# First MLP with one block of 256 tokens, whose products take high and low parts side by side

## The chip, the core and the metric

The kernel runs on one core of a Trainium2 chip. The metric is the device time of one execution in microseconds. Before the change the median of three runs is 883.94 us (883.59 to 884.92). The engines are named as in the profile: PE is TensorE, and PEld its weight loads; DVE is VectorE, ACT is ScalarE, POOL is GpSimd, SP is the engine that issues most DMAs.

## What is computed

```python
def _attn_ref(q, k, v):                      # q, k, v: (4, 8, 576, 64)
    scores = scale * np.matmul(q, k.transpose(0, 1, 3, 2))
    Dmat = np.where(rel >= 0, gamma[:, None, None] ** rel[None, :, :], 0.0)
    return np.matmul(scores * Dmat[None, :, :, :], v)

def _moe_ref(x, w_in, w_out):                # x: (2304, 512), w_in: (512, 2048)
    h = x @ w_in
    g = h * (1.0 / (1.0 + np.exp(-1.702 * h)))
    return g @ w_out

def _moe2_ref(x, w_gate, w_val, w_out, rms_g):   # w_gate: (512, 1536)
    xn = x / np.sqrt(np.mean(x * x, axis=-1, keepdims=True) + 1e-06) * rms_g
    g = xn @ w_gate
    return (g * (1.0 / (1.0 + np.exp(-g))) * (xn @ w_val)) @ w_out
```

The attention's output, as 2304 rows of 512, goes through the first MLP and then through the second. All of it is float32.

## The kernel before

**Number format.** Each float32 operand of an MLP product is split into a high part, rounded to a format that PE takes in one pass, and a low part, the rest. A product is then three matmuls: high x high, high x low, low x high (`three`, lines 277 to 285). The high part comes from an ACT cast, the low part from a DVE (or POOL) subtraction. The weights arrive as float32; ACT rebuilds their words in two steps (lines 189 and 190), DVE joins them (line 243), and then they are split.

**Tiles.** The first MLP goes through the tokens in `BLOCKS`, 512, 384, 384, 512 and 512 of them, and in each block through 16 hidden slices `f` of 128. `m1_up(n, f)` multiplies the block's rows by slice f of `w_in`: four steps of 128 over the model width, three matmuls each, into one PSUM bank `h` of two. ACT takes gelu out of the bank (line 630) and rounds the high part (610), DVE subtracts for the low part (612). `m1_down(n, f)` multiplies the result by slice f of `w_out`, three matmuls for each of four `acc` banks, which collect over all f. Up runs two slices ahead of down (`LAG`).

**Output weights.** `w_rot(n, f)` makes the rounded halves of slice f of `w_out`, in a ring of three: an ACT cast (268) and a DVE subtraction (269), 128x512 whatever the block, while the float32 weights are kept; in block 1 it also stores them (`out_d`), and from slice 13 of block 1 on they are loaded again by a DMA that ACT issues.

**Attention between the products.** The rows of 128 tokens are a unit. Units 0 to 3 are done before the first product; the others run inside the MLP at slices written out in `at_steps`, a list of slices per block: `a_trans(u)` transposes q and k (line 364), and `a_both(u)` does the scores and key-value sums of unit u (396, 405) and the output products of unit u-1 (475). These output products take both `h` banks; ACT copies them out (484), DVE adds (488), and the rows are split by ACT (494) and POOL (495). `a_both(u)` also issues the loads of unit u+1 on SP. In a slice with `a_both`, the down product that is due runs right behind it, ahead of the slice's up product.

**Preparation.** From slice 11 of block 1 on, `make(k)` runs k steps of `prep` per slice: words, joins and splits of the second MLP's gate and value weights. The first two steps are the words of both (four ACT instructions), the next two their joins on DVE, then splits (872, 873), sums on POOL (845).

**Order.** Nothing is scheduled by a planner (`tc.manual_schedule()`): each engine's queue holds its instructions in the order in which this code calls them, each queue runs in order, and semaphores tie the queues.

Of the kernel before, what the change touches and what calls it, by code (L numbers as in the profile page):

```python
# [10 lines left out]
F32 = mybir.dt.float32  # L11
# [7 lines left out]

BLOCKS = (512, 384, 384, 512, 512)  # L20
BLOCKS2 = (768, 768, 768)
XB = 512
TH = 384
# [19 lines left out]
def kernel(  # L43
# [232 lines left out]

    def three(ps, lhs, rhs, first, last, more=False, swap=False):

        (lh, ll), (rh, rl) = lhs, rhs
        pairs = [(lh, rl), (ll, rh)]  # L280
        if swap:
            pairs.reverse()
        nc.tensor.matmul(ps, lh, rh, start=first, stop=False, skip_group_check=more)  # L283
        nc.tensor.matmul(ps, *pairs[0], start=False, stop=False, skip_group_check=more)  # L284
        nc.tensor.matmul(ps, *pairs[1], start=False, stop=last, skip_group_check=more)  # L285

# [70 lines left out]
    def a_trans(u, where):  # L357
# [146 lines left out]

    def wide_scores(u, where, amid=lambda: None):
        qT, kT = st[u]
# [10 lines left out]
        for j in range(2):  # L517
            nc.vector.tensor_tensor(
                out=r[j], in0=sc[j].rearrange("p (a c) -> p a c", c=2 * C),
                in1=wide_mask.unsqueeze(1).to_broadcast([128, HP, 2 * C]), op=ALU.mult,  # L520
            )
            if j == 0:
                amid()
        st[u] = qT, r
# [81 lines left out]
    def g_tile(c):  # L606
        return gp.tile([128, XB], F32, tag="g", name="g", bufs=2)[:, :c]

    def split_hidden(g, gh, gl, fill=lambda: None):
        nc.scalar.copy(out=gh, in_=g)  # L610
        fill()
        nc.vector.tensor_tensor(out=gl, in0=g, in1=gh.bitcast(F32), op=ALU.subtract)  # L612

    def proj(ps, key, f, x, c):
        wh, wl = W[key, f]
        xh, xl = x
        for kk in range(KD):
            three(
                ps,
                (wh[:, kk * 128:(kk + 1) * 128], wl[:, kk * 128:(kk + 1) * 128]),  # L620
                (xh[:, kk, :c], xl[:, kk, :c]),
                kk == 0, kk == KD - 1, swap=key == "in" and f == 0 and c == XB and x is xt.get(0),
            )

    def m1_up(n, f, fill, amid=lambda: None):
        c = BLOCKS[n]
        ps = ps_h.tile([128, XB], F32, tag="h", name="h")[:, :c]
        proj(ps, "in", f, xt[n], c)
        g = g_tile(c)
        nc.scalar.activation(out=g, in_=ps, func=AF.Gelu_apprx_sigmoid)  # L630
        amid()
        G[1, n, f] = hidden_parts(c)
        split_hidden(g, *G[1, n, f], fill)

    def m1_down(n, f):


        def piece(e):
            if f == 0 and e == 0:
                acc[n] = [ps_acc.tile([128, 512], F32, tag="acc", name="acc") for _ in range(4)]  # L640
            wh, wl = R["out", f]
            three(
                acc[n][e][:, :BLOCKS[n]],
                (wh[:, e * 128:(e + 1) * 128], wl[:, e * 128:(e + 1) * 128]),
                G[1, n, f], f == 0, f == NF1 - 1,
            )
            if f == NF1 - 1:
# [13 lines left out]
    def m1_end(n, e):  # L661
# [4 lines left out]
        y = halves([ends[n]], c)[0]  # L666
        (nc.vector.tensor_copy if e % 2 else nc.scalar.copy)(out=y[:, e % 2, :], in_=acc[n][e][:, :c])
        if e % 2:
# [115 lines left out]

    def beside_rows():
        return [t[:, :3, TH:] for t in block_tile(0)]

# [231 lines left out]
    with tc.manual_schedule():  # L1019
# [6 lines left out]
        def a_both(u, where):  # L1026
# [169 lines left out]
        (word, join, wh, wl), (word1, join1, wh1, wl1) = in_halves(0)  # L1196
        word()
        high()
        wide_scores(3, ACC, join)
        wh()  # L1200
        word1()
        low(engine=nc.gpsimd)
# [6 lines left out]
        high(slice(0, 2))  # L1209
        wl()  # L1210
        join1()
        low(slice(0, 2))
        (next_word, join, wh, next_wl), (word2, join2, wh2, wl2) = in_halves(1)
        next_word()
        wh1()
        to_conv.pop(0)
        scaled(1)
        spread_row(nc.gpsimd, qdec, qrow)
        high(slice(2, 4))
        low(slice(2, 4))  # L1220
        for u in range(4):
            a_free(u, "x")
        wl1()
        word2()
# [50 lines left out]
        for n in range(N1):  # L1275
# [19 lines left out]
            for f in range(NF1):  # L1295
# [26 lines left out]
                if (n, f) in ((2, 1), (3, 1), (3, 14)):  # L1322
                    sq = first_load(*{
                        (2, 1): (0, 0, beside_rows()), (3, 1): (0, 1, beside_rows()),
                        (3, 14): (1, 0, in_place(A_WIN)),
# [185 lines left out]
```

## Time and profile before

| | us |
|---|---|
| median of three runs (883.59 to 884.92) | 883.94 |
| the profiled execution | 884.29 |
| its span | 882.6 |
| PE busy | 874.7 |
| DVE busy | 516.1 |
| ACT busy | 382.2 |
| POOL busy | 92.5 |

The span runs from the first to the last instruction; 1.7 us of the profiled execution lie outside it. A busy PE is one that has matmuls in flight: they overlap, so how many it issues in a time is read from the distances of their starts.

### The profile page before, as it was taken

To read this page: it belongs to the slowest core of one execution; us is meant where nothing else is said; L and a number is where in the kernel's file an instruction comes from. 1 tells how busy PE (TensorE), PEld (TensorE's weight loads), DVE (VectorE), ACT (ScalarE), POOL (GpSimd) and SP (SyncE) were. 2 spreads that over 40 slices of the span, in tenths; PEclk is the share of its full clock that TensorE was granted. 3 is DMA by queue.
4 is the path that set the end of the run, shared out by engine and by line. 5 is a ranking of instruction groups with operands and counts; after the bars stand their busy time and mean duration, and the time that the engine had idled before them with its cause. 6 is when DMAs were issued, how large, how long until landed. Compare 5 with 4: busy or idle time off the path is not lost.

```text
span 882.6 us, 16195 instructions
## 1 busy us (share of the span) xinstructions
PE 874.7 (99%) x6176; PEld 789.3 (89%) x6176; DVE 516.1 (58%) x921; ACT 382.2 (43%) x766; POOL 92.5 (10%) x100
## 2 busy tenths in 40 slices
PE   8999999999999999999999999999999999999998
PEld 6788889999999888888889999999999999999997
DVE  4878754474574555756645567765575666333444
ACT  3776753365445554564463343334322215112222
POOL 5100111131232212311200000000000000000000
PEclk9999999999999999999999999999999999999999
DMA  9996444799779987897776676557655556555553
GB/s 209 252 291 197 135 159 159 212 319 317 233 247 316 292 254 237 274 390 262 258 281 219 215 241 209 167 167 267 211 156 158 152 157 224 163 159 157 166 168 107
DMA packets 153584, 193.26 MB, mean 219 GB/s; under 512 B 66656, under 2 KB 94564, under 8 KB 153508
## 3 DMA queue, kind: packets, MB, share of 16 engines
q1 hardware_dynamic: 144596, 164.83, 59.7%
q10 hardware_dynamic: 8688, 27.14, 9.3%
q8 instruction: 49, 0.80, 0.4%
q0 software_dynamic: 224, 0.27, 0.1%
q14 instruction: 27, 0.22, 0.1%
HBM read 149.99 MB, written 42.21 MB: 218 GB/s over the span
## 4 chain that ended last, share of the span: by engine, by line
PE 97%; SPq 1%; DMA 1%; ACT 0%; DVE 0%; issue 0%; DVEq 0%
PE h L285 17%; PE h L283 17%; PE h L284 17%; PE acc L283 11%; PE acc L284 11%; PE acc L285 11%; PE v L285 2%; PE v L284 2%; PE v L283 2%; PE at L475 1%; PE at L364 1%; SPq L339 1%; PE at L396 1%; PE at L405 1%; DMA sslots<-in_moe_w_in_dram 1%; DMA wslots<-in_q_dram 0%
## 5 line engine op out<-in xcount | busy, mean ns | idle before, releaser
L283 PE MATMUL h<-fast 128*128 128x384 f32 (+1 forms) x824 | 288.4, 350 | 0.2 <-ACT fast L589 0.2
L285 PE MATMUL h<-fast 128*128 128x384 f32 (+1 forms) x824 | 287.3, 349 | 0.0
L284 PE MATMUL h<-fast 128*128 128x384 f32 (+1 forms) x824 | 286.7, 348 | 0.1
L922 DVE TENSOR_TENSOR wslots<-h,wslots 128x384 f32<-128x384 f32 x180 | 100.1, 556 | 151.4 <-PE h L285 151.1
L283 PE MATMUL acc<-fast 128*128 128x512 f32 (+1 forms) x464 | 175.0, 377 | 0.0
L285 PE MATMUL acc<-fast 128*128 128x512 f32 (+1 forms) x464 | 174.4, 376 | 0.0
L284 PE MATMUL acc<-fast 128*128 128x512 f32 (+1 forms) x464 | 174.3, 376 | 0.0
L283 PEld LDWEIGHTS h<-fast 128*128 128x128 f32 x824 | 154.7, 188 | 9.9 <-ACT sslots L190 0.4
L284 PEld LDWEIGHTS h<-fast 128*128 128x128 f32 x824 | 154.8, 188 | 9.3 <-DVE fast L218 0.5
L285 PEld LDWEIGHTS h<-fast 128*128 128x128 f32 x824 | 154.6, 188 | 8.2 <-DVE fast L255 0.4
L612 DVE TENSOR_TENSOR fast<-g,fast 128x512 fp32r<-128x512 f32 (+1 forms) x80 | 54.4, 680 | 122.5 <-ACT fast L610 121.8
L955 ACT CAST fast<-g 128x384 fp32r<-128x384 f32 x36 | 18.5, 514 | 219.8 <-DVE g L925 219.8
L630 ACT ACTIVATE g<-h 128x512 f32<-128x512 f32 (+1 forms) x80 | 44.2, 553 | 136.0 <-PE h L285 132.9
L285 PEld LDWEIGHTS acc<-fast 128*128 128x128 f32 x464 | 87.1, 188 | 13.3
L283 PEld LDWEIGHTS acc<-fast 128*128 128x128 f32 x464 | 87.1, 188 | 12.7
L284 PEld LDWEIGHTS acc<-fast 128*128 128x128 f32 x464 | 87.1, 188 | 12.0
L873 DVE TENSOR_TENSOR wslots<-wslots 128x256 fp32r<-128x256 f32 x84 | 43.6, 554 | 15.1 <-ACT wslots L872 14.8
L845 POOL TENSOR_TENSOR wslots<-wslots 128x256 f32<-128x256 f32 x48 | 43.1, 918 | 75.5 <-DVE wslots L243 62.5
L610 ACT CAST fast<-g 128x512 fp32r<-128x512 f32 (+1 forms) x80 | 46.3, 578 | 2.5
L495 POOL TENSOR_TENSOR fast<-x,fast 128x512 fp32r<-128x512 f32 x14 | 18.7, 1339 | 225.6 <-ACT fast L494 225.6
L189 ACT ACTIVATE sslots<-sslots 128x512 f32<-128x512 f32 x56 | 37.8, 675 | 2.3 <-DMA sslots<-in_moe_w_out_dram 2.3
L190 ACT ACTIVATE sslots<-sslots 128x512 uint32<-128x512 uint8 x56 | 37.2, 664 | 0.0
(138 smaller groups left out, 871.0 us busy)
## 6 DMA issues: line engine op xcount, KB each, us to landing
fast<-up_d SPq DMA_DIRECT2D x252, 256.0 KB, 3.0
fast<-out_d ACTq DMA_DIRECT2D x51, 512.0 KB, 5.6
up_d<-wslots SPq DMA_DIRECT2D x84, 256.0 KB, 5.1
sslots<-in_moe_w_out_dram SPq DMA_DIRECT2D x19, 512.0 KB, 5.1
out_d<-fast SPq DMA_DIRECT2D x16, 512.0 KB, 3.7
sslots<-in_moe_w_in_dram SPq DMA_DIRECT2D x15, 512.0 KB, 5.3
sslots<-in_moe_w_val_dram SPq DMA_DIRECT2D x12, 512.0 KB, 6.5
sslots<-in_moe_w_gate_dram SPq DMA_DIRECT2D x11, 512.0 KB, 5.7
```

The costliest lines, as they stand in the source:

```text
L189: nc.scalar.activation(out=hi, in_=hi, func=AF.Prelu, scale=2.0 ** -112, alpha=-(2.0 ** 32))
L190: nc.scalar.activation(out=lo, in_=byte, func=AF.Copy, scale=1 / 32, bias=-31 / 64)
L283: nc.tensor.matmul(ps, lh, rh, start=first, stop=False, skip_group_check=more)
L284: nc.tensor.matmul(ps, *pairs[0], start=False, stop=False, skip_group_check=more)
L285: nc.tensor.matmul(ps, *pairs[1], start=False, stop=last, skip_group_check=more)
L495: nc.gpsimd.tensor_tensor(out=xl, in0=x, in1=xh.bitcast(F32), op=ALU.subtract)
L610: nc.scalar.copy(out=gh, in_=g)
L612: nc.vector.tensor_tensor(out=gl, in0=g, in1=gh.bitcast(F32), op=ALU.subtract)
L630: nc.scalar.activation(out=g, in_=ps, func=AF.Gelu_apprx_sigmoid)
L845: nc.gpsimd.tensor_tensor(out=o, in0=a, in1=b, op=op)
L873: nc.vector.tensor_tensor(out=wl.bitcast(F32R), in0=w, in1=wh, op=ALU.subtract)
L922: nc.vector.tensor_tensor(out=o, in0=a, in1=b, op=ALU.add)
```

## The change

Block 1 has 256 tokens and block 2 has 512. In a block of at most 256 tokens, a high weight part multiplies the rows' high and low parts in one matmul, 256 columns of each side by side in a bank, and the low weight part multiplies the high rows in a matmul of 256 columns (`two`). The two sides are then added: ACT copies the second out of PSUM and DVE adds the first (`joined_sides`), at each up product and at the block's end. `three` keeps one order of its parts; the first product of all has an order of its own, low rows last. Ahead of the first product, the words of the first input weights, their join and their halves are called at other places, and DVE makes qT of unit 3. The attention phases stand at other slices: block 0 holds six phases and block 1 eight, where it was eight and six. `make` runs 2 steps a slice in block 1 (4 before) and 3 in block 2 (2 before).

```diff
-BLOCKS = (512, 384, 384, 512, 512)
+BLOCKS = (512, 256, 512, 512, 512)
...
-            nc.scalar.copy(out=qT, in_=pt[0])
+            (nc.vector.tensor_copy if u == 3 else nc.scalar.copy)(out=qT, in_=pt[0])
...
+        if x is xt.get(0) and key == "in" and f == 0 and not begun:
+            begun.append(f)
+            order = [(kk + k, i, j) for kk in (0, 2) for k, i, j in (
+                (0, 0, 0), (0, 1, 0), (1, 0, 0), (1, 1, 0), (0, 0, 1), (1, 0, 1))]
+            for kk, i, j in order:
+                l, r = parts[kk]
+                nc.tensor.matmul(ps, l[i], r[j], start=(kk, i, j) == order[0], stop=(kk, i, j) == order[-1])
+            return
...
+    def both(at, k, c):
+        return fast[:, at:at + 2 * k * XB].rearrange("p (i k c) -> p k i c", i=2, k=k)[:, :, :, :c]
+
+    def two(bank, lhs, rhs, first, last):
+        c = bank.shape[1] // 2
+        (lh, ll), r = lhs, rhs
+        wide = bank.rearrange("p (i c) -> p i c", i=2)
+        if first:
+            nc.tensor.matmul(wide, lh, r, start=True, stop=False)
+        nc.tensor.matmul(wide[:, 0, :], ll, r[:, 0, :], start=False, stop=False)
+        if not first:
+            nc.tensor.matmul(wide, lh, r, start=False, stop=last)
+
+    def joined_sides(out, bank):
+        c = bank.shape[1] // 2
+        nc.scalar.copy(out=out, in_=bank[:, c:])
+        nc.vector.tensor_tensor(out=out, in0=bank[:, :c], in1=out, op=ALU.add)
...
+        if c <= XB // 2:
+            wh, wl = W["in", f]
+            rows_at = both(n % 2 * 2 * KD * XB, KD, c)
+            for kk in range(KD):
+                ks = slice(kk * 128, kk * 128 + 128)
+                two(ps, (wh[:, ks], wl[:, ks]), rows_at[:, kk], kk == 0, kk == KD - 1)
+            joined_sides(h, ps)
...
+            if BLOCKS[n] <= XB // 2:
+                two(acc[n][e], w, G[1, n, f], f == 0, f == NF1 - 1)
...
+        if c <= XB // 2:
+            joined_sides(y[:, e % 2, :], acc[n][e])
...
-            (2, 3, 4, 6, 8, 10, 12, 14),
-            (1, 3, 5, 7, 9, 10),
+            (2, 3, 4, 6, 9, 12),
+            (0, 2, 4, 6, 8, 10, 12, 14),
...
+        (word, join, wh, wl), (word1, join1, wh1, wl1) = in_halves(0)
+        word()
         a_trans(3, AT)
...
+        join()
         high()
-        wide_scores(3, ACC, join)
+        wide_scores(3, ACC)
         wh()
+        wl()
...
-                    make(2 if n == 2 else 3 if last and f > 5 else 4)
+                    make(2 if n == 1 else 3 if n == 2 or last and f > 5 else 4)
```

PE, block 1, a down product: `acc` are the four banks that collect over the slices, `fast` holds the split operands. Before, two of the four banks:

```order
L283 MATMUL acc_1511<-fast_88 128x384
L284 MATMUL acc_1511<-fast_88 128x384
L285 MATMUL acc_1511<-fast_88 128x384
L283 MATMUL acc_1512<-fast_88 128x384
L284 MATMUL acc_1512<-fast_88 128x384
L285 MATMUL acc_1512<-fast_88 128x384
```

Now, all four banks:

```order
L638 MATMUL acc_1472<-fast_88 128x256
L640 MATMUL acc_1472<-fast_88 128x512
L638 MATMUL acc_1473<-fast_88 128x256
L640 MATMUL acc_1473<-fast_88 128x512
L638 MATMUL acc_1474<-fast_88 128x256
L640 MATMUL acc_1474<-fast_88 128x512
L638 MATMUL acc_1475<-fast_88 128x256
L640 MATMUL acc_1475<-fast_88 128x512
```

Each bank takes two matmuls in place of three, one of them wider and one narrower.

ACT, block 1, from the last of the word instructions at slice 11 to the up product of slice 13 (`g` is the gelu tile, `at` the attention's banks). Before:

```order
L190 ACTIVATE sslots_93<-sslots_93 128x512
L268 CAST fast_88<-wslots_92 128x512
L630 ACTIVATE g_2107<-h_2094 128x384
L610 CAST fast_88<-g_2107 128x384
L872 CAST wslots_92<-wslots_92 128x256 x3
```

Now:

```order
L190 ACTIVATE sslots_93<-sslots_93 128x512
L268 CAST fast_88<-wslots_92 128x512
L368 COPY wslots_92<-at_1936 128x512
L644 COPY g_1949<-h_1948 128x256
L662 ACTIVATE g_1949<-g_1949 128x256
L605 CAST fast_88<-g_1949 128x256
```

The weight cast (268) still stands behind the words; behind it come the kT copy of a unit's transposes and the new copy out of `h`.

DVE, block 1, slices 12 to 14: 243 are the joins, 269 the weight subtraction, 410 (before: 413) the masks of an `a_both`. Before:

```order
L612 TENSOR_TENSOR fast_88<-g_2067,fast_88 128x384
L243 SCALAR_TENSOR_TENSOR wslots_92<-sslots_93 128x512 x2
L269 TENSOR_TENSOR fast_88<-wslots_92,fast_88 128x512
L612 TENSOR_TENSOR fast_88<-g_2107,fast_88 128x384
L873 TENSOR_TENSOR wslots_92<-wslots_92 128x256 x3
```

Now:

```order
L370 TENSOR_TENSOR wslots_92<-at_1935,qdec_102 128x512
L645 TENSOR_TENSOR g_1949<-h_1948,g_1949 128x256
L607 TENSOR_TENSOR fast_88<-g_1949,fast_88 128x256
L243 SCALAR_TENSOR_TENSOR wslots_92<-sslots_93 128x512 x2
L269 TENSOR_TENSOR fast_88<-wslots_92,fast_88 128x512
L645 TENSOR_TENSOR g_1980<-h_1979,g_1980 128x256
L607 TENSOR_TENSOR fast_88<-g_1980,fast_88 128x256
L910 TENSOR_TENSOR wslots_92<-wslots_92 128x256 x2
L410 TENSOR_TENSOR wslots_92<-at_2007,mask_98 128x4x64
L410 TENSOR_TENSOR wslots_92<-at_2008,mask_98 128x4x64
L485 TENSOR_TENSOR x_2069<-at_2043,x_2069 128x128
```

The sums out of `h` (645) stand in the same queue behind the joins and the weight subtraction, and an `a_both` follows in slice 14.

## Rows read from the trace of the kernel before

**Rows 1.** The page, part 1: busy us (share of span) xinstructions.

```profile
PE 874.7 (99%) x6176; PEld 789.3 (89%) x6176; DVE 516.1 (58%) x921; ACT 382.2 (43%) x766; POOL 92.5 (10%) x100
```

**Rows 2.** PE's waits, first and last of six: total us, times, longest.

```profile
PE heat L1106 <- DVE ones L1083: 1.1, 1, 1.1
...
PE h L283 <- ACT fast L589: 0.2, 1, 0.2
```

**Rows 3.** Timeline of PE, block 1: start us, duration us, instruction.

```profile
133.19 0.34 PE L285 MATMUL acc<-fast 128*128 128x384 f32 x1
...
135.76 0.34 PE L284 MATMUL acc<-fast 128*128 128x384 f32 x1
...
137.67 0.33 PE L283 MATMUL h<-fast 128*128 128x384 f32 x1
...
143.74 0.34 PE L285 MATMUL acc<-fast 128*128 128x384 f32 x1
...
144.96 0.34 PE L284 MATMUL h<-fast 128*128 128x384 f32 x1
```

**Rows 4.** Timeline of PE, block 3, 512 tokens.

```profile
295.87 0.39 PE L283 MATMUL h<-fast 128*128 128x512 f32 x1
...
303.80 0.39 PE L285 MATMUL acc<-fast 128*128 128x512 f32 x1
```

**Rows 5.** Groups by line and shape: xcount | busy us, mean ns | idle before.

```profile
L269 DVE TENSOR_TENSOR fast<-wslots,fast 128x512 fp32r<-128x512 f32 x26 | 22.1, 850 | 2.6 <-ACT fast L268 2.2
...
L484 ACT COPY x<-at 128x256 f32<-128x256 f32 x28 | 9.0, 375 | 26.4 <-PE at L475 26.4
...
L413 DVE TENSOR_TENSOR wslots<-at,mask 128x256 f32<-128x256 f32 x28 | 10.5, 418 | 8.9 <-PE at L405 8.9
...
L215 ACT CAST fast<-ww 128x256 fp32r<-128x256 f32 x4 | 1.5, 402 | 2.4 <-DVE ww L209 2.4
...
L243 DVE SCALAR_TENSOR_TENSOR wslots<-sslots 128x512 uint32<-128x512 uint32 x36 | 24.2, 684 | 2.5 <-ACT sslots L190 2.5
...
L189 ACT ACTIVATE sslots<-sslots 128x512 f32<-128x512 f32 x56 | 37.8, 675 | 2.3 <-DMA sslots<-in_moe_w_out_dram 2.3
```

**Rows 6.** Timelines of PE, ACT, DVE and POOL, block 1; [idle before <-releaser].

```profile
174.87 0.33 PE L283 MATMUL h<-fast 128*128 128x384 f32 x1
...
175.06 0.49 ACT L630 ACTIVATE g<-h 128x384 f32<-128x384 f32 x1 [3.65 <-PE h L285]
...
176.00 0.62 ACT L494 CAST fast<-x 128x512 fp32r<-128x512 f32 x1
...
178.09 0.67 ACT L189 ACTIVATE sslots<-sslots 128x512 f32<-128x512 f32 x1
...
180.32 0.63 ACT L268 CAST fast<-wslots 128x512 fp32r<-128x512 f32 x1
...
177.18 1.36 DVE L269 TENSOR_TENSOR fast<-wslots,fast 128x512 fp32r<-128x512 f32 x1 [0.48 <-ACT fast L268]
...
176.70 1.29 POOL L495 TENSOR_TENSOR fast<-x,fast 128x512 fp32r<-128x512 f32 x1 [12.62 <-ACT fast L494]
...
136.41 0.49 DVE L488 TENSOR_TENSOR x<-at,x 128x128 f32<-128x128 f32 x2 [1.00 <-ACT x L484]
```

**Rows 7.** DMA issues by line: xcount, KB each, median us to landing.

```profile
wslots<-in_q_dram SPq DMA_DIRECT2D x30, 128.0 KB, 4.4
```

**Rows 8.** Timelines of PE, ACT, DVE and SP's issues, start and block 0.

```profile
24.31 0.50 PE L283 MATMUL h<-fast 128*128 128x512 f32 x1 [0.16 <-ACT fast L589]
...
44.25 0.68 ACT L189 ACTIVATE sslots<-sslots 128x512 f32<-128x512 f32 x1 [2.28 <-DMA sslots<-in_moe_w_out_dram]
...
49.99 0.69 DVE L255 TENSOR_TENSOR fast<-ww,fast 128x512 fp32r<-128x512 f32 x1
...
50.10 0.47 PE L283 MATMUL h<-fast 128*128 128x512 f32 x1
...
33.20 4.79 SPq L339 DMA_DIRECT2D wslots<-in_q_dram  x2
```

More of the change, by code (lines that the diff above doesn't have):

```diff
@@ L275, in w_rot, with three @@
         R["out", f] = (wh, wl)
-    def three(ps, lhs, rhs, first, last, more=False, swap=False):
+    def three(ps, lhs, rhs, first, last, more=False):
         (lh, ll), (rh, rl) = lhs, rhs
-        pairs = [(lh, rl), (ll, rh)]
-        if swap:
-            pairs.reverse()
         nc.tensor.matmul(ps, lh, rh, start=first, stop=False, skip_group_check=more)
-        nc.tensor.matmul(ps, *pairs[0], start=False, stop=False, skip_group_check=more)
-        nc.tensor.matmul(ps, *pairs[1], start=False, stop=last, skip_group_check=more)
+        nc.tensor.matmul(ps, lh, rl, start=False, stop=False, skip_group_check=more)
+        nc.tensor.matmul(ps, ll, rh, start=False, stop=last, skip_group_check=more)
     C = 64
@@ L503, with wide_scores @@
     wide_mask = sp.tile([128, TH], F32, tag="norm", name="wide_mask", bufs=3)[:, :2 * C]
[L505 removed]
+    def wide_scores(u, where):
         qT, kT = st[u]
@@ L612, in split_hidden @@
         nc.vector.tensor_tensor(out=gl, in0=g, in1=gh.bitcast(F32), op=ALU.subtract)
+    begun = []
     def proj(ps, key, f, x, c):
@@ L616, in proj @@
         xh, xl = x
[L617 to L623, printed above, removed]
+        parts = [((wh[:, kk * 128:(kk + 1) * 128], wl[:, kk * 128:(kk + 1) * 128]), (xh[:, kk, :c], xl[:, kk, :c]))
+                 for kk in range(KD)]
+        if x is xt.get(0) and key == "in" and f == 0 and not begun:
[6 more added lines that the diff above has]
+            return
@@ new lines, in proj @@
+        for kk, (l, r) in enumerate(parts):
+            three(ps, l, r, kk == 0, kk == KD - 1)
+    def both(at, k, c):
[9 more added lines that the diff above has]
+            nc.tensor.matmul(wide, lh, r, start=False, stop=last)
@@ L631, in m1_up @@
         amid()
+        at = A_HID + n_hid[0] % 3 * 1024
         G[1, n, f] = hidden_parts(c)
         split_hidden(g, *G[1, n, f], fill)
+        if c <= XB // 2:
+            G[1, n, f] = both(at, 1, c)[:, 0]
     def m1_down(n, f):
@@ L640, in piece @@
                 acc[n] = [ps_acc.tile([128, 512], F32, tag="acc", name="acc") for _ in range(4)]
[L641 to L646, printed above, removed]
+            w = [t[:, e * 128:(e + 1) * 128] for t in R["out", f]]
+            if BLOCKS[n] <= XB // 2:
+                two(acc[n][e], w, G[1, n, f], f == 0, f == NF1 - 1)
+            else:
+                three(acc[n][e][:, :BLOCKS[n]], w, G[1, n, f], f == 0, f == NF1 - 1)
             if f == NF1 - 1:
@@ L666, in m1_end @@
         y = halves([ends[n]], c)[0]
-        (nc.vector.tensor_copy if e % 2 else nc.scalar.copy)(out=y[:, e % 2, :], in_=acc[n][e][:, :c])
+        if c <= XB // 2:
+            joined_sides(y[:, e % 2, :], acc[n][e])
+        else:
+            (nc.vector.tensor_copy if e % 2 else nc.scalar.copy)(out=y[:, e % 2, :], in_=acc[n][e][:, :c])
         if e % 2:
@@ L781, in norm_steps, with beside_rows @@
         ]
-    def beside_rows():
-        return [t[:, :3, TH:] for t in block_tile(0)]
+    def beside_rows(n):
+        return [t[:, :3, TH:] for t in block_tile(n)]
     def in_place(at):
```

24 lines of the change are left out of this document (11 added, 13 removed).

## The prediction

> **What bounds the kernel now.** The page's first part is read first: PE is busy for 99% of the span [rows 1]. PE's own waits come next: six in all, the longest 1.1 us, all before the first product of the MLP [rows 2]. So from the first product to the last, PE never stands still; its instructions, one after another, are the time. The change can gain only by giving PE less to issue, and it loses whatever makes PE wait, at once and in full.
>
> I call U(f) and D(f) the up and the down product of hidden slice f in token block 1, 16 slices in all. "Both" is one unit's attention scores with another's output, "trans" a unit's transposes.
>
> **Fewer matmuls.** Matmuls start at even distances: 36 of 384 columns from 137.67 to 143.74 us, 0.1734 us each [rows 3]; 36 of 512 columns from 295.87 to 303.80, 0.2266 each [rows 4]. The 128 columns between cost 0.0532, so 512 cost 0.2128, and 0.0138 of each matmul is independent of its width. Block 1 goes from 16 slices x 24 matmuls of 384 to 16 x 16, half of 512 and half of 256; block 2 goes from 384 matmuls of 384 to 384 of 512. The columns are the same in sum, 128 matmuls fall away: 128 x 0.0138 = **1.8 us saved**. A 256-column matmul would then start 0.2266 - 2 x 0.0532 = 0.120 after the one before. No row has one of this kind. Its upper bound is the 0.173 of the 384s [rows 3], should the loading of the next weights set the distance; that adds 128 x 0.053 = 6.8 us. Its lower bound is the columns alone, 0.106, another 1.8 saved. I take 0.120: the line through two widths already holds whatever a load of 128 columns costs in every matmul.
> The Trainium skill (TensorE: Matmul & The Clock Gate, Back-to-back issue gap) has another overhead: the columns at the full clock plus 2.5 ns. By it the saving would be 0.3 us, an estimate, and my sum 1.5 us higher; the distances of these rows exceed it, and they decide.
>
> **What the narrow block asks of the other engines.** U and D take 4 x (0.227 + 0.120) = 1.39 us each, where they took 2.08. Per slice the work behind them does not shrink alike: the rounding of the output weights stays 128x512 (ScalarE cast 0.62, VectorE subtract 0.69 to 1.36 [rows 5, 6]), and a ScalarE copy and a VectorE sum of 128x256 out of PSUM are new (0.38 and 0.42 by the nearest forms [rows 5]). The chain from U's end to its finished halves becomes: 0.19 until ScalarE starts (174.87 to 175.06 [rows 6]), copy 0.38, sum 0.42, gelu about 0.40, cast 0.40, subtract 0.42, some 2.3 us; before, 1.8. The bank of U is free only after the sum, so a VectorE queue that is late now holds PE directly: through the bank, through G and through the rounded weights. Also, block 1 now holds four trans and four boths, the last at slice 14, where block 1 had its last at slice 10.
>
> Costs of the attention to PE: both 133.19 to 135.76 less two distances = 2.22 us; trans 143.74 to 144.96 less two = 0.87 [rows 3]. They are moved, not added: nothing.
>
> **Where PE waits: slices 11 to 14**, counted from U(10)'s end as 0. PE wants U(11), D(9), trans, U(12), D(10), U(13), D(11) at 0, 1.39, 2.77, 3.65, 5.03, 6.42, 7.81, then the scores of the both at 9.2 and its output products at 10.3.
> - The other side: copy(10) 0.2, sum to 1.0, gelu, cast to 1.9, cast of the attention rows (0.62) to 2.4, weight cast(10) to 3.0. GpSimd's subtract of these rows (1.29 at 176.70) runs beside VectorE's weight subtract(10), which then takes 1.36, as at 177.18 [rows 6]: to 4.35. Sum(11) to 4.75, gelu and cast(11) to 5.6.
> - Here ScalarE has the four conversions of the first gate and value weights before the weight cast(11): 178.09 to 180.32, 2.23 us [rows 6]. Cast(11) 7.75 to 8.4, subtract(11) to 9.1. **D(11) wants it at 7.8: 1.3 us of wait.** In the kernel before, the same four stood there and slices were longer.
> - Then kT copy, copy(12) to 9.2, qT product on VectorE to 9.75, sum(12) 10.1, gelu, cast, subtract(12) 11.4; two joins (0.68 each [rows 5]) to 12.6; weight subtract(12) 13.25; sum(13) 13.6. The output products of the both take both `h` banks, and the second is U(13)'s: **wanted at 11.6, free at 13.65: 2.05 us.**
> - Behind them VectorE has subtract(13), two splits and two masks (some 0.4 each by [rows 5]) before the sum of the attention rows that frees the bank for U(14): 16.7 against 16.1, **0.6 us**.
> That is 3.95; with the contended subtract at 0.69, 3.3. At slices 6 and 10 the both alone does it: before, the two sums of the attention rows (0.49 from 136.41 [rows 6]), which free the banks, ended 1.1 us after the D behind the both had begun to flow at 135.76 [rows 3], and it lasts 2.08; now D is 1.39 and VectorE comes there later: 0 to 0.35 each. I take **4.0 us** together, ends 2 (each operation at its start-to-start distance, nothing contended) and 6 (all contended, gelu and casts late too).
>
> **Loads of q.** From a both to the next trans PE has 4 x 1.39 = 5.5 us, 8.3 before. Four issues and a landing of 4.4 us median [rows 7] need about that: 0 to 0.5 for each of three, of which PE's waits above give most back. Taken as 0, 1.0 in the upper end.
>
> **The start.** Words ahead of the transposes, the join ahead of both masks, and a first product that uses its low parts last let the first product begin some 0.5 us before 24.31 [rows 8], and the second up to 1.1 us earlier, since the first no longer waits inside. It is given back: at 44.25 ScalarE waits for an output-weight load, and behind it in order stand the words of input slice 5, whose low half VectorE makes at 49.99; PE starts that product at 50.10 [rows 8] with nothing in hand. The load is paced by SP's issues, themselves stuck for 4.8 us at 33.20 [rows 8], not by PE. Taken as 0; ends -1.1 and 0.
>
> The VectorE qT copy of unit 3 and the moved phases of block 0 stand beside longer work there: nothing. Blocks 2 to 4 have slices of 5.4 us and at most the preparation that block 3 carried without a wait: nothing.
>
> **Sum.** -1.8 + 4.0 = +2.2 us. The profiled execution took 884.29 us and would become 886.5; the median is 0.35 below it, so 883.94 + 2.2 = **886.2 us**.
>
> **Rivals.**
> - *The queue is less late* (0.22). If GpSimd's subtract misses VectorE's weight subtract(10) and operations start before the former's end, as the four conversions do (2.23 us for four of 0.67 [rows 5, 6]), the waits come to 2 to 2.6: 884.1 to 884.8, no change. For it: such overlap; against: chains across engines have none.
> - *The queue does not reach PE* (0.12), the other side: the whole 1.8 stays, 882.1. It decides at two points: subtract(11) done by 7.8 and sum(13) by 10.3 after U(10). My count is 1.3 and 3.3 late there, so it needs a chain much shorter than any row gives.
> - *The start is kept* (0.08): if the load that ends the wait at 44.25 lands earlier too, 1.1 of the forecast goes: 885.1.
> - *Weights set the distance* (0.08): 256 columns at 0.173 cost 6.8; each U and D is 0.21 longer, so the waits shrink to some 2.5: 883.94 - 1.8 + 6.8 + 2.5 = 891.4. Against it: the straight line above.
> That the built program does other than the diff says, its order excludes.
>
> **Chances.** The forecast has 0.50, own range 885.0 to 888.5. About 0.2% (1.8 us) is what a measurement of this kernel can tell from no change: 882.2 to 885.7. Slower: 0.44 of the forecast, half of the kept start, the weights: 0.56. Same: 0.06 of the forecast, 0.20 of the first rival, 0.03 and 0.04 of the next two: 0.33. Faster: 0.09 and 0.02: 0.11. The range runs from the saving alone, 882.1, to waits of 6 and loads of 1, 889.1.
>
> **What would show it.** Matmul starts in block 1 at 0.227 and 0.120; PE's waits no longer at the start alone but at D(11) for VectorE's weight subtract, at the attention output products of slice 14 for a bank, 1 to 2 us each; the first product at about 23.8 us, slice 5 still near 50.1. I am wrong if PE shows no wait in block 1, or if the 256-column distance is over 0.13.

## The result, and the profile of the changed kernel

The changed kernel takes **890.81 us** (median of six runs, 889.66 to 892.16), the kernel before 883.90 beside it (883.55 to 884.92): a ratio of 1.0077, interval 1.0066 to 1.0088. It is 6.9 us slower. The forecast was 886.2, with a range up to 889.1: the sign was right, the size was not. The profiled execution took 890.52 us, span 888.8, against 884.29 and 882.6.

The page of the changed kernel, part 1 (compare [rows 1]):

```profile
PE 875.7 (99%) x6048; PEld 767.1 (86%) x6048; DVE 521.9 (59%) x940; ACT 387.3 (44%) x783; POOL 89.3 (10%) x100
```

128 matmuls are gone, as the diff says, and PE is still "busy 99%". The loss is in PE's waits: total us, times, longest.

```profile
PE at L361 <- DMA wslots<-in_k_dram: 1.6, 1, 1.6
PE at L472 <- DVE g L645: 1.6, 1, 1.6
PE heat L1143 <- DVE ones L1120: 1.1, 1, 1.1
PE acc L638 <- DVE fast L269: 1.1, 1, 1.1
PE at L361 <- DMA wslots<-in_q_dram: 1.0, 2, 0.6
PE h L280 <- ACT fast L605: 0.7, 2, 0.4
```

These are the first six of eleven rows; the others are 0.5 us or less. Before, all waits of note lay ahead of the first product [rows 2]. Here all but the `heat` one of these six lie inside the first MLP. L638 is a narrow matmul of a down product, L472 the attention output products, L361 the transposes of q and k, L280 the first matmul of an up product.

**The time, place by place.** Three marks, the first matmul of an up product each, from the timelines of PE, and the end of the span:

| us | before | after | difference |
|---|---|---|---|
| first product | 24.31 | 23.82 | -0.49 |
| block 0, slice 5 | 50.10 | 49.67 | -0.43 |
| block 3, slice 3 | 295.87 | 302.35 | +6.48 |
| end of the span | 882.6 | 888.8 | +6.2 |

So all of it arises in blocks 0 to 2, where the time from the first product to slice 3 of block 3, the first mark to the third here, goes from 271.56 to 278.53 us, 6.97 more. The distance of each matmul's start from the next one's is compared with the prediction's straight line (0.0138 us and 0.4157 ns for each column); what exceeds it is listed here (the first row is the count of matmuls times 0.0138):

| us | forecast | measured |
|---|---|---|
| 128 matmuls fewer | -1.8 | -1.77 |
| D(11), for the weight subtraction | 1.3 | 1.24 |
| slice 14, output products, for an `h` bank | 2.05 | 1.70 |
| U(14), for its bank | 0.6 | 0 |
| behind the boths of slices 6 and 10, for a bank | 0 to 0.7 | 0.79 |
| transposes of unit 11 in block 2, for k and q | 0 | 2.35 |
| block 0, up products of slices 8 and 14, for their input weights | 0 | 1.02 |
| block 0, slice 2, for unit 4's q | 0 | 0.75 |
| single matmuls that start late, behind a stop, an attention phase or a late weight half, 36 for 30 | 0 | 0.60 |
| wide and narrow matmuls off the line | 0 | 0.33 |
| waits of before that are gone | 0 | -0.43 |
| sum | 2.2 | 6.6 of 6.97 |

The other 0.4 us stay unplaced. One trace stands behind each column, and the start differs from execution to execution: from the first product to slice 5 the changed kernel took 25.85 us, and the ten experiments below with the same start took 25.22 to 26.40; unit 4's q cost them 0 to 0.83. So in the experiments a difference of the marks below some 1 us is read from slice 5 on, which takes 245.77 us before and 252.68 in the changed kernel.

The foreseen waits at D(11) and slice 14, and the one for unit 11's loads, can be read in the timeline of PE (start, duration, instruction, idle before and its releaser):

```profile
168.08 0.40 PE L640 MATMUL h<-fast 128*128 128x512 f32 x1
169.55 0.38 PE L638 MATMUL acc<-fast 128*128 128x256 f32 x1 [1.07 <-DVE fast L269]
...
173.97 0.63 PE L472 MATMUL at<-wslots 64*64 64x64 f32 x27 [1.58 <-DVE g L645]
...
182.35 0.63 PE L361 MATMUL at<-ident,wslots 128*128 128x128 f32 x4 [1.64 <-DMA wslots<-in_k_dram]
183.36 0.63 PE L361 MATMUL at<-ident,wslots 128*128 128x128 f32 x4 [0.38 <-DMA wslots<-in_q_dram]
```

From 168.08 to 169.55 is 1.47 us where 0.23 is due: D(11). The second wait is slice 14's. The last two rows are the one that the prediction set to nothing: unit 11's loads.

What is late before D(11) shows in the chain of waits (start, duration, what):

```profile
163.44 1.35 DVE fast L269
164.79 0.34 DVE g L645
...
166.02 0.58 ACT sslots L189
...
167.72 0.55 ACT sslots L190
168.27 0.52 ACT fast L268
```

It is the chain of the forecast, link by link: the weight subtraction at 1.35 beside GpSimd, four word instructions of 2.24 us on ACT, then the weight cast. What holds block 0 was not in it. In the timeline of the changed kernel, slice 5 first, then slice 8 (`ww` is the joined word of the input weights; the casts and subtractions out of it are their high and low halves):

```profile
49.67 0.46 PE L280 MATMUL h<-fast 128*128 128x512 f32 x1
49.97 0.62 ACT L605 CAST fast<-g 128x512 fp32r<-128x512 f32 x1
...
65.41 1.37 DVE L269 TENSOR_TENSOR fast<-wslots,fast 128x512 fp32r<-128x512 f32 x1 [0.35 <-ACT fast L268]
66.18 1.50 POOL L350 TENSOR_TENSOR wslots<-wslots,vdec 128x512 f32<-128x512 f32 x1
66.70 1.53 DVE L243 SCALAR_TENSOR_TENSOR ww<-sslots 128x512 uint32<-128x512 uint32 x1
68.26 0.43 DVE L252 CAST fast<-ww 128x512 fp32r<-128x512 f32 x1
68.72 0.69 DVE L255 TENSOR_TENSOR fast<-ww,fast 128x512 fp32r<-128x512 f32 x1
68.83 0.47 PE L280 MATMUL h<-fast 128*128 128x512 f32 x1 [0.35 <-ACT fast L605]
69.47 0.19 PEld L282 LDWEIGHTS h<-fast 128*128 128x128 f32 x1 [0.37 <-DVE fast L255]
```

The up product of slice 8 waits for the halves of its own input weights: its first matmul starts 0.14 us after the high half is done at 68.69, and the weight load of its third stands 0.37 us until the low half is done at 69.41. The row names ACT's L605 (the cast of slice 7), which ended at 68.74 and so came last by the profile; but slice 5's up product began at 49.67, before the cast of slice 4 had begun (49.97), so an up product doesn't need that cast; and the bank that it takes, slice 6's, had been read out by 63.68. The halves are late because ACT works without a pause from 63.08 to 68.75, the words of these weights behind a gelu and three casts (of the slice, the attention rows and the output weights), and because VectorE's subtraction (269) and join (243) take 1.37 and 1.53 us beside GpSimd's operations. Before, the same was so:

```profile
67.13 1.53 DVE L243 SCALAR_TENSOR_TENSOR ww<-sslots 128x512 uint32<-128x512 uint32 x1
68.76 1.03 PE L364 MATMUL at<-ident,wslots 128*128 128x128 f32 x8
69.55 0.48 PE L283 MATMUL h<-fast 128*128 128x512 f32 x1
```

But a trans stood in slice 8, and the up product began 0.79 us behind the down product's end; now the trans stands in slice 9. In slice 14 it is the both of before that is gone.

### The profile page after: what moved, and what is told of

It is laid out like the page before. It is cut to its first block, busy times and chain, and to the rows that moved or that the text cites. A ratio compares the mean times of both kernels' runs of the same rounds, so it can differ in the third digit from the quotient of the medians.

```text
span 888.8 us, 15953 instructions
## 1 busy us (share of the span) xinstructions
PE 875.7 (99%) x6048; PEld 767.1 (86%) x6048; DVE 521.9 (59%) x940; ACT 387.3 (44%) x783; POOL 89.3 (10%) x100
## 4 chain that ended last, share of the span: by engine, by line
PE 91%; DMA 3%; ACT 3%; SPq 2%; DVE 1%; issue 1%; DVEq 0%
PE h L280 16%; PE h L282 16%; PE h L281 16%; PE acc L280 10%; PE acc L281 10%; PE acc L282 10%; PE v L282 2%; PE v L281 2%; PE v L280 2%; DMA wslots<-in_q_dram 1%; PE at L472 1%; SPq L336 1%; PE at L361 1%; DMA sslots<-in_moe_w_out_dram 1%; PE at L393 1%; PE h L640 1%
## 5 line engine op out<-in xcount | busy, mean ns | idle before, releaser
L280 PE MATMUL h<-fast 128*128 128x384 f32 (+1 forms) x756 | 268.7, 355 | 0.7 <-ACT fast L605 0.7
L282 PE MATMUL h<-fast 128*128 128x384 f32 (+1 forms) x756 | 267.8, 354 | 0.0
L281 PE MATMUL h<-fast 128*128 128x384 f32 (+1 forms) x756 | 267.0, 353 | 0.0
L280 PE MATMUL acc<-fast 128*128 128x512 f32 x400 | 156.6, 392 | 0.0
L282 PE MATMUL acc<-fast 128*128 128x512 f32 x400 | 156.6, 391 | 0.0
L281 PE MATMUL acc<-fast 128*128 128x512 f32 x400 | 156.4, 391 | 0.0
L280 PEld LDWEIGHTS h<-fast 128*128 128x128 f32 x756 | 141.9, 188 | 12.9 <-ACT fast L605 1.5
L282 PEld LDWEIGHTS h<-fast 128*128 128x128 f32 x756 | 141.9, 188 | 11.1 <-DVE fast L255 1.3
L281 PEld LDWEIGHTS h<-fast 128*128 128x128 f32 x756 | 141.9, 188 | 11.0
L662 ACT ACTIVATE g<-h 128x512 f32<-128x512 f32 x64 | 38.2, 596 | 119.2 <-PE h L282 116.6
L282 PEld LDWEIGHTS acc<-fast 128*128 128x128 f32 x400 | 75.0, 188 | 15.8
L280 PEld LDWEIGHTS acc<-fast 128*128 128x128 f32 x400 | 75.1, 188 | 14.7
L281 PEld LDWEIGHTS acc<-fast 128*128 128x128 f32 x400 | 75.1, 188 | 14.3
L605 ACT CAST fast<-g 128x512 fp32r<-128x512 f32 (+1 forms) x80 | 46.2, 578 | 2.5
L882 POOL TENSOR_TENSOR wslots<-wslots 128x256 f32<-128x256 f32 x48 | 40.7, 866 | 60.2 <-DVE wslots L243 59.2
```

What stands on the lines that cost most here:

```text
L281: nc.tensor.matmul(ps, lh, rl, start=False, stop=False, skip_group_check=more)
L282: nc.tensor.matmul(ps, ll, rh, start=False, stop=last, skip_group_check=more)
L662: nc.scalar.activation(out=g, in_=h, func=AF.Gelu_apprx_sigmoid)
L882: nc.gpsimd.tensor_tensor(out=o, in0=a, in1=b, op=op)
```

## The experiments

Times beside the kernel before on the same chip (883.8 to 884.1 there). "Between the marks" is the time of the table above from the first product to slice 3 of block 3: 271.56 us before, 278.53 after.

**e1: the trans of unit 11 one slice later** (the row of block 2 in `at_steps`).

```
-            (0, 2, 4, 6, 8, 10, 12, 14),
+            (1, 2, 4, 6, 8, 10, 12, 14),
```

> The changed kernel with one number moved: the first trans of block 2 (unit 11) stands at slice 1 in place of slice 0; its both stays at slice 2. Theory (loads): PE stands 1.8 us at that trans because unit 11's k and q are issued on SP only behind slice 14's both, and 0.6 us more inside it; with one slice of 5.4 us more the loads have landed, so 2.2 to 2.5 us go: about 888.4 us in all. Rival (queues): the ACT and DVE queues left late by slice 14 are what PE meets there, the loads only come last by a little; then the wait moves to the up product of block 2's first slices and the time stays at 890.8. In between, 889: the copies of kT and qT, now one slice before the scores, make the both at slice 2 wait some 0.5 us.

889.47 us, ratio 1.0065 (1.005 to 1.008); 276.50 between the marks. The loads' 2.35 us are gone, and this is new:

```profile
PE h L281 <- POOL fast L492: 0.6, 1, 0.6
```

The first product of block 2 now waits 0.8 us for the low rows of unit 9, which GpSimd makes behind slice 14's both. The loads had covered it. Both theories hold a part: 2.35 taken, 0.8 given back; from slice 5 on it is 251.15 us, 1.53 less. The time fell by 1.3 us, where 2.2 to 2.5 were expected.

**e2: no preparation in block 1.**

```
-                if n > 1 or n == 1 and f > 10:
-                    make(2 if n == 1 else 3 if n == 2 or last and f > 5 else 4)
+                if n > 1:
+                    make(4 if n == 2 else 3 if last and f > 5 else 4)
```

> The changed kernel without the preparation of the second MLP's weights in block 1; block 2 runs 4 steps a slice in place of 3 and makes up for it. Theory (queue late from slice 11): without the four word instructions on ACT and the two joins on DVE, D(11) no longer waits (1.25 us now) and the output products of slice 14 wait 0.4 us at most (1.70 now), as the boths of slices 2 and 6 do: 2.5 to 3.0 us less, about 888.0; the wait for unit 11's loads stays. Rival (the both and the joined sides do it alone): the waits lose at most 1 us together, 889.8 or more. Second rival: 4 steps a slice are too many for block 2, new waits there of 1 us and more, 889 to 891.

886.44 us, ratio 1.0028 (1.0017 to 1.0040); 274.50 between the marks. D(11) and slice 14 do not wait at all; block 2 shows no new wait. PE's waits from 120 to 185 us:

```profile
PE at L361 <- DVE g L645: 0.9, 1, 0.9
PE at L361 <- DMA wslots<-in_q_dram: 0.6, 1, 0.6
PE h L637 <- DVE x L485: 0.5, 2, 0.2
```

So the both and the sum of the two sides alone do not make slice 14 wait; the preparation in the same slices does. The loads of unit 11 are late without it too: the first row names DVE, which had long been done, and k landed at 177.80, where the transposes begin. The gain is larger than the 2.5 to 3.0 us expected: 4.4 in the time, 3.7 from slice 5 on (248.96). Some 0.4 of it is a shorter wait for these loads (1.93 for 2.35); without preparation the next weights on SP are loaded behind them.

**e5: the same, but the four word instructions stay at slice 11.**

```
-                if n > 1 or n == 1 and f > 10:
-                    make(2 if n == 1 else 3 if n == 2 or last and f > 5 else 4)
+                if n > 1 or n == 1 and f == 11:
+                    make(2 if n == 1 else 4 if n == 2 else 3 if last and f > 5 else 4)
```

> The changed kernel with the preparation in block 1 cut to its first two steps, the four word instructions on ACT at slice 11; the two joins on DVE and all that follows move to block 2, at 4 steps a slice. Theory (ACT's words hold D(11), DVE's joins hold slice 14): D(11) still waits 1.2 us; the sum out of the bank of slice 13 comes 1.4 us earlier, so the output products of slice 14 wait 0.4 to 0.6 in place of 1.8; the transposes of unit 11 wait for its loads as before. Some 889.5 in all. Rival (the words make everything behind them late, the joins lie in slack): slice 14 still waits 1.2 or more, 890.5. Other end (slice 14's wait needs both, and D(11)'s goes with it): 887.5.

888.57 us, ratio 1.0051 (1.0038 to 1.0063). PE's waits from 160 to 185 us:

```profile
PE at L361 <- DMA wslots<-in_q_dram: 1.7, 1, 1.7
PE acc L638 <- DVE fast L269: 1.1, 1, 1.1
PE at L472 <- DVE g L645: 0.6, 1, 0.6
```

ACT's words hold D(11); DVE's joins, with the splits behind them that this edit moves too, hold 1.0 of slice 14's 1.6. The forecast had given the joins 1.4 of 2.05.

**e3: other places for the phases.**

```
-            (2, 3, 4, 6, 9, 12),
-            (0, 2, 4, 6, 8, 10, 12, 14),
+            (2, 3, 4, 6, 8, 12, 14),
+            (0, 2, 4, 6, 8, 10, 12),
```

> The changed kernel with the attention phases at other slices: block 0 at 2, 3, 4, 6, 8, 12, 14 (the second trans back at 8, the third added at 14), block 1 at 0, 2, 4, 6, 8, 10, 12, so that its last both stands at 12 in place of 14 and unit 11's loads are issued two slices earlier. Theory: in block 0, PE's two waits for ACT's queue at the up products of slices 8 and 14 (0.51 us each and 0.3 for the three slow matmuls behind each) come from a slice without a trans two slices behind a both; both go, 1.6 us. The loads of unit 11 have landed at the trans of block 2, 2.4 us. In block 1 slice 10 carries a trans and no both, so GpSimd's subtraction does not meet the weight subtraction, and the both of slice 12 is ahead of the joins: 1 to 2 of the 3 us of waits go. Together 5 to 6: 885 to 886. Rival for block 0 (ACT has too much there whatever the order): its waits move to other slices, 887. Rival for block 1 (every both in a narrow block costs what slice 14's did): 888.

888.35 us, ratio 1.0056 (1.0041 to 1.0071), where 885 to 886 was expected; 275.75 between the marks. Block 0 did as expected: with a trans back in slice 8 and one in slice 14, both waits of its up products are gone. Unit 11's loads land in time. But the wait for loads came back at slice 10, at the transposes of unit 10:

```profile
148.71 0.43 SPq L169 DMA_DIRECT2D sslots<-in_moe_w_gate_dram  x1
149.19 0.90 SPq L169 DMA_DIRECT2D sslots<-in_moe_w_val_dram  x1
150.18 1.21 SPq L336 DMA_DIRECT2D wslots<-in_k_dram  x2
151.48 3.16 SPq L336 DMA_DIRECT2D wslots<-in_q_dram  x2
```

On SP the first weights of the second MLP (two transfers of 512 KB, at slice 8 by the code) now stand ahead of unit 10's k and q; q took 6.23 us to land and PE waited 1.9. D(11) still waited 1.18, and a down product 0.65 for a reload of output weights. The time is that of the rival for block 1 (888), the cause is not: loads in the place of queues. That the two large transfers make q late is read from their order; no run moves them alone.

**e9: without the reloads of output weights in block 1.**

```
-        else:
+        elif n > 1:
             nc.scalar.dma_start(out=both.bitcast(F32), in_=out_d[f])
```

> The changed kernel without the loads of the stored output weights in block 1: slices 13 to 15 of that block multiply whatever the ring holds, so three transfers of 512 KB are left out, and with them part of the computation. Everything else, unit 11's loads behind slice 14's both too, is as in the changed kernel. Theory (the transfers share the 16 engines): unit 11's k and q, which took 7.3 and 6.5 us from issue to landing, land after 4.0 to 5.2 us, and the waits of PE at its transposes fall from 2.35 us in all to 0.3 to 1.2; 1.2 to 2 us faster, some 889.2. Rival (the four loads are slow by themselves, or issued too late): they still take 6 us and more and the waits keep 2 us; 890.5.

888.71 us, ratio 1.0050 (1.0037 to 1.0063); 275.39 between the marks. The transposes of unit 11 no longer wait (0.16 us against 2.35), and from slice 5 on it is 250.14, 2.5 less. DMA issues from 172 to 178 us (xcount, KB each, median us to landing), the changed kernel first:

```profile
fast<-out_d ACTq DMA_DIRECT2D x1, 512.0 KB, 6.3
wslots<-in_k_dram SPq DMA_DIRECT2D x2, 128.0 KB, 7.3
wslots<-in_q_dram SPq DMA_DIRECT2D x2, 128.0 KB, 6.6
```

Then this experiment:

```profile
wslots<-in_k_dram SPq DMA_DIRECT2D x2, 128.0 KB, 4.3
wslots<-in_q_dram SPq DMA_DIRECT2D x2, 128.0 KB, 4.0
```

The theory holds: 512 KB a slice, which ACT issues, make SP's loads land 2.6 to 3 us later. Weights of the second MLP stand ahead on SP too (issued at 169.90 and 170.38 in the changed kernel, 169.15 and 169.63 here); they stay in this run, so without the reloads they don't hold k and q. The Trainium skill (DMA: Bandwidth & Descriptors, Issuing engines are not separate DMA queues) says that transfers issued by several engines run on the same 16 DMA engines and interleave; these rows agree.

**e4: the two sides stored next to each other**, so that the wide matmul reads one run of 512 (rows and hidden halves of the narrow block); of the edit, the rows' view:

```
-        return fast[:, at:at + 2 * k * XB].rearrange("p (i k c) -> p k i c", i=2, k=k)[:, :, :, :c]
+        return fast[:, at:at + k * XB].rearrange("p (k i c) -> p k i c", i=2, k=k)
```

> The changed kernel with the narrow block's high and low rows, and its hidden halves, stored next to each other, so that the wide matmul of 512 columns reads one run of 512 in place of two runs of 256 that lie apart; same columns, same order. The distance from a wide matmul to the narrow one behind it is 0.233 us in the changed kernel, 0.227 between two matmuls of 512 elsewhere. Theory (two runs): the jump between the runs costs the 7 ns; 128 such matmuls, 0.9 us less, 889.9, distance 0.227. Rival (the alternation of widths costs it): distance stays 0.233, 890.8.

891.07 us, ratio 1.0086 (1.0069 to 1.0103). The median distance from a wide matmul to a narrow one is still 0.233 us, as the rival had it. The two runs are not the cause; whether the alternation of widths is, e10 asks.

**e6: the repaired kernel**, put together from the above: e2's `make`, and

```
-                if n == 1 and f == 8:
+                if n == 1 and f == 9:
...
-            (2, 3, 4, 6, 9, 12),
-            (0, 2, 4, 6, 8, 10, 12, 14),
+            (2, 3, 4, 6, 8, 12, 14),
+            (0, 3, 4, 7, 8, 11, 12),
```

> The changed kernel with what the first four experiments point to: no preparation in block 1 (4 steps a slice in block 2), the second MLP's first weights loaded at slice 9 of block 1 in place of 8, and the phases at 2, 3, 4, 6, 8, 12, 14 in block 0 and 0, 3, 4, 7, 8, 11, 12 in block 1: three slices from each both (with the loads of the next unit) to the next trans, four before the one of block 2. Theory (the changed kernel is the kernel before plus waits): the two waits of block 0 (1.6 with what follows them), D(11) and slice 14 (3.0) and the loads (2.4, 1.9 in the run without preparation) go; up to 0.4 at each of three boths stays. The first products up to the fourth of block 3 take 271 to 271.5 us, 278.5 in the changed kernel and 271.6 in the one before; time 883.0 to 884.0. Rival (a narrow block's slices are too short for the queues and loads whatever the order): new waits of 2 us and more, 885.5 or above. Other end (everything hidden, the 1.8 us are kept): 882.2.

885.01 us, ratio 1.0011 (1.0002 to 1.0020), 1 us above the expected time and still slower than the kernel before; 272.77 between the marks, 1.3 above the expectation. PE's waits from 120 to 190 us:

```profile
PE at L393 <- DVE wslots L370: 0.6, 2, 0.3
PE acc L637 <- ACT sslots L704: 0.4, 1, 0.4
PE acc L638 <- DMA fast<-out_d: 0.2, 1, 0.2
```

Everything large is gone. What is left is the price of a trans directly ahead of its both (L370 makes qT), the end of block 0, and a reload. By the distances of the starts, the waits over 0.2 us from 120 to 190 us come to 2.5 us in seven places, more than the change saves.

**e7: the repaired kernel with three narrow matmuls** in place of a wide and a narrow one; no sums of two sides. The conditions that choose the new form never hold; beside e6's edit:

```
-        if c <= XB // 2:
+        if c < 0:
...
-            if BLOCKS[n] <= XB // 2:
+            if BLOCKS[n] < 0:
```

> The repaired kernel (no preparation in block 1, phases spread), with the narrow block's products as three matmuls of 256 columns in place of one of 512 and one of 256; no sum of two sides any more. It measures the side-by-side form alone and the distance of two matmuls of 256. Theory (straight line): 256 behind 256 starts after 0.120 us; a product of four pairs takes 1.44 in place of 1.40, 32 such products 1.2 us more; the queues of ACT and DVE lose 0.8 us a slice, so that up to 1 us of the waits left at the boths goes: 0.2 to 1.2 us slower than the repaired kernel. Rival (a floor for narrow matmuls, such as the 0.173 of 384 columns or something in between): at 0.130 the 384 matmuls take 3.8 us more, at 0.173 20 us more.

887.49 us, ratio 1.0029 (1.0017 to 1.0040), but the eleven runs lie between 883.95 and 888.76. The straight line holds: in the timeline of PE narrow matmuls start 0.12 apart.

```profile
125.96 0.28 PE L281 MATMUL h<-fast 128*128 128x256 f32 x1
126.08 0.28 PE L282 MATMUL h<-fast 128*128 128x256 f32 x1
```

The rest, in the profiled execution (887.98 us), is a late reload of output weights in this order of the queues, and what it did to PE's clock. The windows of the profiled execution (us, busy us of PE, PEld, DVE, ACT, POOL, then the granted clock, the DMA share and GB/s):

```profile
179.00:181.50 2.50, 0.33 (x2) 0.00 (x0) 0.69 (x1) 2.10 (x4) 0.00 (x0) 1.00 1.01 395
181.50:184.00 2.50, 2.31 (x12) 2.34 (x13) 1.38 (x2) 1.37 (x3) 0.33 (x1) 0.58 0.28 109
184.00:186.00 2.00, 2.00 (x8) 1.68 (x8) 0.00 (x0) 0.00 (x0) 1.12 (x2) 0.67 0.32 57
```

PE waits 2.36 us for the reload; behind it the granted clock falls, and narrow matmuls start 0.21 apart until 184.20, wide ones 0.43. The twelve narrow ones alone take 2.51 us in place of 1.44. The five runs at a mean clock of 0.999 or 1.0 took 883.95 to 886.52 (median 885.15, e6 885.01), the six at 0.997 or 0.998 took 887.49 to 888.76. Of the eleven, the profiled one alone, one of the six, has a trace; that the wait for the reload makes the difference in the others is not shown. The form "side by side" could not be told from three narrow matmuls by the time.

**e8: the repaired kernel with the old start**, of which the core is:

```
-        (word, join, wh, wl), (word1, join1, wh1, wl1) = in_halves(0)
-        word()
         a_trans(3, AT)
...
+        (word, join, wh, wl), (word1, join1, wh1, wl1) = in_halves(0)
+        word()
         high()
```

> The repaired kernel with the start of the kernel before: words, joins and halves of the first input weights where they were, unit 3's qT on ACT, the first product in its old order. It measures the new start alone. The five traces with the new start have the first up product at 23.59 to 24.07 us and the sixth (slice 5) at 49.13 to 50.17, the kernel before 24.31 and 50.10. Theory (most is given back by the load that paces slice 5): first product at 24.3, slice 5 at 49.7 to 50.2, time 0 to 0.4 us above the repaired kernel, not to be told apart. Rival (the gain is kept): slice 5 at 50.1 where the repaired kernel has 49.4 or earlier, 0.7 us and more slower.

885.89 us, ratio 1.0018 (1.0009 to 1.0027), 0.88 above e6 on the same chip: with eleven runs of each, that difference can be told (resampled, 0.1 to 1.4). First product at 24.28, slice 5 at 49.81, third mark at 297.06, against 23.63, 49.09 and 296.40 in e6: 0.65, 0.72 and 0.66 us. So between these two the gain of the start is kept, as the rival had it. Over all traces the new start has slice 5 between 49.06 and 50.17, the old one at 50.10 and 49.81: some 0.4 us on average, and nothing in the latest.

**e10 and e11: wide and narrow matmuls in pairs** (wide, narrow, narrow, wide), e11 with the phases of block 1 at 0, 2, 4, 6, 8, 10, 12. The core of the edit, beside e6's:

```
-        if first:
+        lead = first or lead and not last
+        if lead:
```

> The repaired kernel (885.0 us) with the wide and narrow matmuls of the narrow block in another order: wide, narrow, narrow, wide, wide, narrow and so on, so that half of the changes of width go. Theory (the change from wide to narrow costs 7 ns, gives 3 back from narrow to wide): wide to wide 0.227, narrow to narrow 0.120 as in the run of three, half of the pairs at 0.347 in place of 0.351; 0.2 to 0.3 us less, within the spread of the times. Rival (the wide matmul of this block is slow whatever follows): wide to wide at 0.233 too, nothing gained.

885.37 us, ratio 1.0016 (1.0008 to 1.0024): no gain. The rival was right: a wide matmul takes 0.233 also ahead of a wide one, a narrow one 0.117 also ahead of a narrow one. Why they leave the line there (0.227 and 0.120) stays open: neither the two runs (e4) nor the change of width (here) does it.

> The same order of matmuls, with the phases of block 1 two slices apart (0, 2, 4, 6, 8, 10, 12) in place of 0, 3, 4, 7, 8, 11, 12: a trans is two slices ahead of its both, and the loads of a unit have two slices in place of three. In the repaired kernel PE waits 0.43 and 0.48 us at two boths for the products of the trans one slice ahead, and 0.2 in three other places of block 1. Theory (each spacing has its wait): these two go, the bank waits of 0.4 behind the boths come back at two or three places, the loads land 0.5 us ahead or behind: 884.5 to 885.3, no better than the kernel before. Rival (the spacing was all that was left): the waits of block 1 go, 883.5 or less, faster than both. Other side (loads too late again at two slices): waits of 1.5 us, 886.5.

884.11 us, ratio 0.9998 (0.9986 to 1.0009): no difference from the kernel before can be told. That is between the theory (884.5 to 885.3) and the rival (883.5 or less): the two waits at the boths went, a bank wait and a reload stayed. PE's waits from 120 to 185 us are down to two:

```profile
PE acc L639 <- DMA fast<-out_d: 0.6, 1, 0.6
PE h L638 <- DVE x L485: 0.3, 1, 0.3
```

Of all versions run, this is the best form of the change. It is level with the kernel before, not ahead: 1.77 us saved less 0.33 off the line are 1.44, and by the distances of the starts three waits of 1.4 us together are left here from 150 to 181 us (0.73 of it for a reload).

## Why the prediction was wrong

**Right.** The saving, 1.77 us by the count and 1.44 with the distances as they are; narrow matmuls at 0.117 to 0.120; PE's waits at D(11) and at slice 14 with their causes and nearly their sizes (2.94 for 3.35, and 3.73 for all of block 1's queue waits where 4.0 was taken); e2 and e5 take them away one by one as the count had it. That the sum fits so well is in part luck: U(14) did not wait (0.6 forecast), and two boths behind which a bank was late waited 0.4 each, a little above the 0.35 given.

**Wrong: "Loads of q. Taken as 0, 1.0 in the upper end".** This is the largest miss, 2.35 us. The step took four issues and the median landing of 4.4 us [rows 7] against 5.5 us of products, for three pairs of both and trans inside block 1; the fourth, from slice 14's both to unit 11's trans in block 2, had no term. At slices 2, 6 and 10 that was right (the last q landed 0.5 to 1.5 us ahead of the transposes). At the block's end it was not: there the reloads and stores of output weights move 512 KB each a slice, slices had become shorter, k took 7.3 us, and PE waited for k as well as for q. A median over the whole kernel was used for a stretch whose DMA engines were full (share 1.04 from 174 to 180 us in the changed kernel). The kernel before had the same transfers there, but slices of 4.2 us and none of a unit's loads beside them: its last both stood at slice 10. e9 shows the cause, e1 the price.

**Wrong: "the moved phases of block 0 stand beside longer work there: nothing".** The trans that left slice 8 had put the up product off by 0.79 us, in which its input weights were finished; the both that left slice 14 did the same there. The prediction asked what the new places cost, not what the old place had hidden. 1.0 us at two slices, gone in e3 with a trans in each again.

**Wrong: a wait was priced at its own length.** Behind a stop the first matmul's distance is some 0.1 us longer, and where the low half of the weights is late as well, three are (0.31, 0.33 and 0.34 us in place of 0.227 from 68.83 on; the product at 50.10 before did so already). The sum had no term for it. 0.6 us more than before.

**Mis-sized: the start.** "Taken as 0" holds for the average no better than half: the traces have 0.4 us at slice 5 (-0.43 here), and e8 against e6 has 0.66 us kept to the third mark and 0.88 in the time. On the way PE waited 0.59 us for unit 4's q, since it came there earlier, and lost 0.75 with what follows; that was not in the sum, but in five of the other ten traces with this start it is nothing, so it belongs to this execution more than to the change.

**The range.** Its upper end added waits of 6 and loads of 1. The waits of block 1 and 2 with loads came to 6.1; block 0's 1.0, unit 4's q, slow matmuls behind waits and the matmuls off the line had no place in it. The rival "weights set the distance", 891.4, would have given nearly this time by another cause; the distances exclude it.

## What to carry to other kernels

When a block is made narrower, everything that comes once a slice whatever the width (weights, their reloads, attention loads) comes that much faster: price each load by the landing time of its own stretch, with the transfers of all engines that fall there. When a phase moves, ask what the old place was hiding as well as what the new one costs. A saving of 0.2% on the busiest engine is worth less than one wait of 2 us, so first list every buffer and load that the shorter slices want sooner.

## What the runs showed of the hardware

- The first matmul behind a stop of PE keeps the next one waiting for some 0.1 us more than its distance: D(11)'s narrow one at 169.55 us is followed at 169.78, 0.23 us later in place of 0.12. So does the first product matmul behind an attention phase, where PE had not stopped: in the changed kernel 75.40 to 75.71 behind a trans, 0.31 in place of 0.227, then 0.23. The granted clock is 1.00 in both places. In the timeline of PE:

```profile
75.40 0.48 PE L280 MATMUL h<-fast 128*128 128x512 f32 x1
75.71 0.40 PE L281 MATMUL h<-fast 128*128 128x512 f32 x1
```

- A wait for weights can stand in the rows of the weight loads alone: at 69.47 us PEld had been idle for 0.37 us until the low half came, and PE's own row shows no idle time, since the matmul before it was still in flight.
- VectorE's join of two operands (243) took 1.53 us beside a GpSimd operation of 1.50, and 0.68 at 60.17 us with none beside it; its weight subtraction (269) took 1.37 and, at 59.56 us, 0.69.
- After waits of 1.6 us the granted clock stayed at 1.00 in the changed kernel's trace; after 2.36 us in e7 it fell to the lower of its two levels, 1.2 GHz, and stayed there until some 185.4 us (means of 0.58 and 0.67 in the windows), though PE was busy again. The Trainium skill (TensorE: Matmul & The Clock Gate, What's actually happening) says that the clock is granted by how busy PE has been recently, which agrees with the stop and the fall in e7's windows. Two of the six runs of the changed kernel had a mean clock of 0.998 and took 892.05 and 892.16 us, the four at 1.0 889.66 to 890.86; the two have no trace.
- In the narrow block a wide matmul took 0.233 us and a narrow one 0.117, off the line by +7 and -3 ns in every order tried.
